# Random-feature attention with a gated layer: an account of engine times orders attention and its filling; row maxima in PSUM

## The chip, the cores and the metric

The kernel runs on one core of one Trainium2 chip. The metric is the device time of one execution in microseconds (us), median of several runs. The core's engines are named as in the profile: PE (matrix products; PEld are its weight loads), DVE (vector), ACT (scalar), POOL (GpSimd) and SP (here only a queue that issues DMAs). Each engine works through its own instructions in the order in which they stand in the program, and waits where an operand is not there yet.

## The reference

```
# q, k, v: [8, 8, 576, 64]; omega: [128, 64]
def phi(x):                                   # x = q or k, divided by 64 ** 0.25
    h = einsum('bhsd,md->bhsm', x, omega) - sum(x * x, -1, keepdims=True) / 2
    return exp(h - max(h, -1, keepdims=True)) / sqrt(128)
kv = einsum('bhsm,bhsd->bhmd', phi(k), v);  z = sum(phi(k), axis=2)
attn = einsum('bhsm,bhmd->bhsd', phi(q), kv) / (phi(q) . z + 1e-6)
x = attn, tokens by heads: [4608, 512]
out = (sigmoid(x @ w_gate) * (x @ w_val)) @ w_out      # d_ff = 1536; the three w are float64
```

## The kernel before

All products are float32. An operand of a large product is split into a rounded high part and the rest ("hi", "lo"), and three products of such parts stand for one (PE reads them as fp32r). The work has four stages.

**Attention** (`norms`, `projected`, `keys`, `queries`; L493 to L671). A unit `u` is two batches, 1152 tokens, 9 tiles of 128; there are 4 units, 4 pairs of heads `p`, and two halves `b` of a unit, one per batch. A task of `norms` loads token tiles (`nat`), squares them on ACT (`x2`) and sums them on DVE (`ss`, then `sq`). A task of `keys` or `queries` loads `raw`, splits it (ACT writes `hi`, POOL writes `lo`), and multiplies by omega on PE into a PSUM bank `pp`. DVE takes the row maxima `mx` (L552) and forms `hm` (L556). For keys, DVE forms `nb` (L574), ACT does the exponentials `kp` (L587), and PE sums `pkv` (L595) with the values `v`. For queries, DVE forms `sub` and `h` (L613, L615), PE transposes `h` into `pt`, ACT does `qp` (L628), PE multiplies by `kv` into `pn` (L638), DVE divides (`den`, `inv`, `x`: L643 to L649), PE transposes into `px` (L655), ACT copies to `xs` and issues the store of `xT` to DRAM (L663).

**First pass** (`first_pass`, L227): for each chunk of 512 tokens (the first in two halves), `load` brings `xr` from `xT`, ACT and POOL split it (`xe`), and PE makes gate and value of four of the twelve column tiles, 12 matmuls each (`gv`, L247); 80 such products ("wholes") in all. Once a chunk is split and its weights are there they depend on nothing in attention, so they are what PE can do while attention waits: the filling. **Conversion** (`from_float64`, `first_weights`, `convert_weights`; tiles `e`, `c`): six DVE instructions and one on POOL turn 512 columns of float64 weights into float32, 36 times; the later weights get four POOL subtractions and go back to DRAM (`w32`).

**Second pass** (`second_pass`, `gated`, L333): the other eight column tiles by a scheme of seven block products, into banks `gw`, 72 groups of 42 matmuls, three banks each. **Last** (L443): the product with w_out by the same scheme, into four banks `po` per block of 256 tokens, 18 blocks of 126 matmuls.

What sets the order before: the tasks are taken round robin by `attention` (L681), at most 6 at once. While the program is written, a counter gives attention 10 to 14 steps for each half product of the first pass, and one conversion step at a time from then on (L721 to L739). A scheduler of the framework then reorders all of it on every engine by its own estimate of when operands are there, except for what `pin` holds in place, which is the second pass and what belongs to it. PSUM has 8 banks: 6 with the tag `at` and 2 with `gv`; in the later stages `any_bank` takes three `at` and one `gv` in turn.

Of the kernel before, what the change touches and what calls it, by code (L numbers as in the profile page):

```python
# [45 lines left out]
AT_ONCE = 6  # L46
AHEAD = 8
EVERY = 32
FROM = 20
RATE = 14  # L50
FIRST = 10

RAWS, SPLITS, KPS, VS, HS, XS = 6, 5, 8, 3, 4, 3
# [13 lines left out]

def split(nc, hi, lo, x, lo_engine=None):

    nc.scalar.activation(out=hi, in_=x, func=AF.Copy)  # L70
    (lo_engine or nc.vector).tensor_tensor(out=lo, in0=x, in1=hi.bitcast(F32), op=ALU.subtract)  # L71


def from_float64(nc, t, a, bits):
# [3 lines left out]
    nc.vector.tensor_scalar(out=a, in0=hi, scalar1=0x7FFFFFFF, scalar2=None, op0=ALU.bitwise_and)  # L78

# [15 lines left out]
    x = t.bitcast(F32)
# [4 lines left out]
def attn_glu_kernel(ctx: ExitStack, tc, qT, kT, qn, kn, va, om, ident, w, out):  # L100
    nc = tc.nc
# [36 lines left out]
    def converted(cv, i):  # L138


        raw = [cv[:, (1 + h) * 2 * WP : (2 + h) * 2 * WP] for h in range(2)]
        for h in range(2):
            o = i + h * WP
            nc.sync.dma_start(out=raw[h].rearrange("p (n two) -> p n two", two=2), in_=w[:, o : o + WP, :])
        yield
        for h in range(2):
            from_float64(
                nc, cv[:, h * WP : (h + 1) * WP], cv[:, 6 * WP :],
                raw[h].rearrange("p (n two) -> p n two", two=2),
            )  # L150
            yield

    def first_weights(pool, tiles):

        for j in range(NE):
            cv = tiles(f"e{j}")
            ws[j] = wh, wl = [pool.tile([P, WE], F32R, name=f"{t}{j}") for t in ("wh", "wl")]
            steps = converted(cv, j * WE)
            next(steps)
            for i in range(2):  # L160
                next(steps)
                s = slice(i * WP, (i + 1) * WP)
                split(nc, wh[:, s], wl[:, s], cv[:, s].bitcast(F32), lo_engine=nc.gpsimd)
                yield

    def convert_weights(tiles, ns):

        for n in ns:
            cv = tiles(f"c{n}")
            for _ in converted(cv, NE * WE + n * 4 * Q):  # L170
                yield
# [9 lines left out]
            nc.sync.dma_start(out=w32[n], in_=f)  # L181
# [45 lines left out]
    def first_pass():  # L227


        def parts_of(o, n, at):  # L230
            raw = load(o, n)
            yield
# [5 lines left out]
        def product(i, j, o, n, x):  # L238
            name = f"gv{o}_{j}_{i}"
            gv = (any_bank(name) if late else bank("gv", name))[:, :n]  # L240
            wh, wl = ws[j]
            m = 0
            for k in range(KC):
                s = slice((i * KC + k) * P, (i * KC + k + 1) * P)
                xh, xl = x[k][:, 0], x[k][:, 1]
                for u, v in ((wl, xh), (wh, xl), (wh, xh)):
                    nc.tensor.matmul(gv, lhsT=u[:, s], rhs=v, start=(m == 0), stop=(m == 3 * KC - 1))  # L247
                    m += 1
            return gv
# [616 lines left out]
```

## Time and profile before

| | us |
|---|---|
| median of three runs (1235.72 to 1240.33) | 1237.9 |
| the profiled execution, whole | 1239.43 |
| its span, first to last instruction | 1237.6 |
| first matmul of the first pass (`gv`) starts at | 65.1 |
| last copy of attention (`xs`) starts at | 508.5 |
| last `gv` matmul starts at | 585.1 |
| second pass | 585 to 958 |
| last | 958 to 1238 |
| busy, of the span: PE, DVE, ACT, POOL | 1172.3, 864.5, 530.7, 542.7 |

The stages overlap in their beginnings. PE counts as busy from a matmul's start to its modelled end, and matmuls are pipelined, so that a busy PE may run well below its rate; how close they follow each other says more. PEclk in a row of the profile is the share of PE's full clock that it was granted.

### The profile page before, as it was taken

The page shows a single profiled execution, that of the slowest core. Times are in us where ns is not written, and L with a number is a line of the kernel's source. Part 1 is how long each engine was busy: PE and PEld are TensorE (multiplying, and loading weights), DVE is VectorE, ACT ScalarE, POOL GpSimd, SP SyncE. Part 2 cuts the span into 40 slices and gives each one's busy share as a digit, 9 for nine tenths or more (in the row PEclk, how much of TensorE's full clock was granted, in tenths as well). Part 3 has the DMA queues.
Part 4 walks back from the last instruction along what each step waited for, and adds up shares of the span by engine and source line. Part 5 has one row for each costly group of instructions (what it writes and reads, how often), then busy time and mean ns, then how long its engine had stood idle before and what let it go on. Part 6 is the DMA issues. An engine that isn't in the chain of part 4 may idle for free.

```text
span 1237.6 us, 23990 instructions
## 1 busy us (share of the span) xinstructions
PE 1172.3 (95%) x8828; PEld 1109.8 (90%) x8828; DVE 864.5 (70%) x1907; ACT 530.7 (43%) x1164; POOL 542.7 (44%) x599
## 2 busy tenths in 40 slices
PE   6798989999898999899899999999998899999998
PEld 5788978798887888788899999999998899999998
DVE  4889888999698866433566656666569777777773
ACT  5556755565455463342423322232325344343331
POOL 2454365556457552131466666666666211111110
PEclk7798989999899999899899999999999999999999
DMA  7667767786657641461432333323337676666662
GB/s 247 213 199 228 210 219 253 238 268 237 226 182 252 223 153 39 139 202 52 152 128 106 123 135 124 121 93 125 124 135 267 203 226 195 188 191 189 198 191 94
DMA packets 104950, 219.43 MB, mean 177 GB/s; under 512 B 11136, under 2 KB 42112, under 8 KB 103040
## 3 DMA queue, kind: packets, MB, share of 16 engines
q1 hardware_dynamic: 87984, 198.94, 48.5%
q10 hardware_dynamic: 16848, 18.95, 4.4%
q8 instruction: 70, 1.15, 0.4%
q14 instruction: 48, 0.39, 0.1%
HBM read 141.82 MB, written 76.02 MB: 176 GB/s over the span
## 4 chain that ended last, share of the span: by engine, by line
PE 71%; DVE 12%; issue 7%; DMA 5%; POOL 3%; ACT 1%; SPq 1%; ACTq 0%; DVEq 0%; POOLq 0%
PE gw L351 27%; PE po L465 20%; PE gv L247 10%; PE pkv L595 4%; PE pnq L638 4%; PE ptq L626 2%; DVE mxq L552 2%; DVE hq L615 1%; DMA xr<-xT 1%; DMA xT<-xsq 1%; DMA rawk<-kT 1%; POOL loq L71 1%; DVE hmq L556 1%; PE ppk L547 1%; POOL xe L71 1%
## 5 line engine op out<-in xcount | busy, mean ns | idle before, releaser
L351 PE MATMUL gw<-xl,u 128*128 128x256 f32 x3024 | 364.6, 283 | 6.9 <-ACT p L362 3.6
L351 PEld LDWEIGHTS gw<-xl,u 128*128 128x128 f32 x3024 | 363.5, 191 | 7.9 <-DVE u L331 3.9
L465 PE MATMUL po<-u,yh 128*128 128x256 f32 x1512 | 272.4, 283 | 0.0
L465 PEld LDWEIGHTS po<-u,yh 128*128 128x128 f32 x1512 | 234.8, 191 | 0.0
L465 PE MATMUL po<-u,yl 128*128 128x256 f32 x756 | 214.0, 283 | 3.3 <-DVE yl L71 3.3
L247 PE MATMUL gv<-xe,wh 128*128 128x512 f32 (+1 forms) x640 | 201.0, 388 | 2.1 <-POOL xe L71 2.1
L70 ACT ACTIVATE yh<-yr 128x896 fp32r<-128x896 f32 x108 | 100.2, 950 | 156.8 <-PE po L465 86.3
L465 PEld LDWEIGHTS po<-u,yl 128*128 128x128 f32 x756 | 144.3, 191 | 3.9 <-DVE yl L71 3.9
L247 PEld LDWEIGHTS gv<-xe,wh 128*128 128x128 f32 x640 | 117.3, 194 | 20.1 <-POOL xe L71 4.5
L71 POOL TENSOR_TENSOR yl<-yr,yh 128x896 fp32r<-128x896 f32 x17 | 38.0, 2232 | 215.3 <-PE po L465 139.9
L247 PE MATMUL gv<-xe,wl 128*128 128x512 f32 (+1 forms) x320 | 125.8, 394 | 2.7 <-POOL wl L71 1.6
L71 DVE TENSOR_TENSOR yl<-yr,yh 128x896 fp32r<-128x896 f32 x91 | 103.0, 1144 | 31.5 <-PE po L465 19.1
L331 DVE TENSOR_TENSOR u<-gw,p 128x256 f32<-128x256 f32 x144 | 60.7, 422 | 59.2 <-PE gw L351 51.1
L595 PE MATMUL pkv<-v,kpk 128*128 128x66 f32 x512 | 84.4, 290 | 13.3 <-ACT kpk L587 12.6
L595 PEld LDWEIGHTS pkv<-v,kpk 128*128 128x128 f32 x512 | 77.0, 209 | 21.5 <-ACT kpk L587 19.8
L71 POOL TENSOR_TENSOR lok<-rawk,hik 128x256 fp32r<-128x256 f32 (+1 forms) x80 | 55.5, 712 | 68.0 <-ACT hik L70 67.6
L456 DVE TENSOR_TENSOR yr<-yr 128x128 f32<-128x128 f32 x144 | 60.1, 451 | 35.3 <-DMA yr<-ye 34.8
L71 POOL TENSOR_TENSOR xe<-xr,xe 128x512 fp32r<-128x512 f32 (+1 forms) x40 | 49.1, 1244 | 74.2 <-ACT xe L70 62.4
L71 POOL TENSOR_TENSOR loq<-rawq,hiq 128x256 fp32r<-128x256 f32 (+1 forms) x80 | 56.5, 718 | 55.5 <-ACT hiq L70 54.7
L587 ACT ACTIVATE kpk<-ppk,nb 128x128 f32<-128x128 f32 x256 | 69.8, 393 | 17.4 <-DVE nb L574 17.1
L638 PEld LDWEIGHTS pnq<-kv,qpq 128*128 128x128 f32 (+1 forms) x640 | 70.5, 189 | 6.5 <-ACT qpq L628 4.3
L638 PE MATMUL pnq<-kv,qpq 128*128 128x66 f32 (+1 forms) x640 | 74.9, 273 | 1.4 <-ACT qpq L628 1.2
(108 smaller groups left out, 2166.6 us busy)
## 6 DMA issues: line engine op xcount, KB each, us to landing
yl<-yl SPq DMA_DIRECT2D x36, 896.0 KB, 3.8
yr<-yl SPq DMA_DIRECT2D x72, 448.0 KB, 3.5
xr<-xT SPq DMA_DIRECT2D x68, 256.0 KB, 4.7
c<-w SPq DMA_DIRECT2D x28, 512.0 KB, 5.1
w<-c SPq DMA_DIRECT2D x14, 1024.0 KB, 4.5
v<-va SPq DMA_DIRECT2D x32, 330.0 KB, 3.4
natk<-kn SPq DMA_DIRECT2D x36, 256.0 KB, 4.2
natq<-qn SPq DMA_DIRECT2D x36, 256.0 KB, 3.9
```

The source lines that it names most:

```text
L70: nc.scalar.activation(out=hi, in_=x, func=AF.Copy)
L71: (lo_engine or nc.vector).tensor_tensor(out=lo, in0=x, in1=hi.bitcast(F32), op=ALU.subtract)
L247: nc.tensor.matmul(gv, lhsT=u[:, s], rhs=v, start=(m == 0), stop=(m == 3 * KC - 1))
L331: return nc.vector.tensor_tensor(out=o, in0=a, in1=b, op=ALU.add)
L351: nc.tensor.matmul(o, lhsT=u[:, k, s], rhs=v[:, kc, :], start=(first and m == 0), stop=(m == 5), skip_group_check=not first,)
L456: nc.vector.tensor_tensor(out=raw[:, o], in0=raw[:, a], in1=raw[:, b], op=op)
L465: nc.tensor.matmul(o, lhsT=u[:, i, :], rhs=v[:, k, :], start=(j + m == 0 and n in (1, 6, 5, 4)), stop=(j == NPAIR - 1 and m == 2), skip_gr ...
L552: nc.vector.tensor_reduce(out=m.rearrange("p t h -> p (t h)"), in_=pp, axis=AX.X, op=ALU.max)
L587: nc.scalar.activation(out=kp[t][:, h, :], in_=pp[:, 2 * i + h, :], func=AF.Exp, bias=nb[:, t - t0, h : h + 1], scale=SCALE,)
L595: nc.tensor.matmul(pkv[:, h, :], lhsT=kp[b * MID + i][:, h, :], rhs=v[:, i, h, :], start=(i == 0), stop=(i == MID),)
L626: nc.tensor.transpose(out=pt[:, i, :], in_=h_sb[:, i, :], identity=id_sb)
L638: nc.tensor.matmul(pn[r, 2 * i + h, :], lhsT=qp[:, 2 * i + h, r], rhs=kvs[u, p, bb][:, h, :], start=True, stop=True,)
```

## The change

Only the stretch in which attention, the first pass and the conversions are mixed is written anew, and the bank tags. The arithmetic is the same.

1. `Clock` keeps, while the program is made, a time per engine and per tile: each instruction that is recorded moves its engine's time on by a fixed part and a part per element, a tile is due at its writer's end, a DMA's target 2.5 us after it is recorded. It also keeps apart the DVE instructions that read two SBUF operands (or run at double rate) and the POOL instructions, which it lets not overlap.
2. Every step of a task now says which engine it goes to and when its operands are due. `attention` records, in this order of preference: a step of ACT, DVE or POOL that is due; a conversion step, if DVE is free; a PE step of attention that has been due for 0.5 us; three matmuls of the first pass; a PE step that is just due; else it moves the account on. Older tasks go first. `fill` puts single conversion instructions between dependent small DVE instructions.
3. This stretch is written with `manual_schedule`, so that PE, DVE, ACT and POOL keep exactly the recorded order. SP's queue is still the framework's.
4. At most 62 of the 80 wholes are placed in this stretch (LEFT = 18).
5. `mx` and `hm` move from SBUF tiles to one PSUM bank, `small`; `at` keeps 5 banks, `gv` 2, also for the second pass and the last stage.
6. Tasks at once 6 to 7, `norms` up to 20 tasks ahead; buffers SPLITS 5 to 6, KPS 8 to 6, XS 3 to 4. The first four weight loads are issued first of all.

```diff
-AT_ONCE = 6
-AHEAD = 8
+AT_ONCE = 7
+AHEAD = 10
+LEFT = 18
+MARGIN = 0.5
+QUEUED = 2.0
-RAWS, SPLITS, KPS, VS, HS, XS = 6, 5, 8, 3, 4, 3
+RAWS, SPLITS, KPS, VS, HS, XS = 6, 6, 6, 3, 4, 4
+class Clock:
+    COST = {
+        "PE": (0.013, 1 / 2400, 0.27), "ACT": (0.1, 0.00082, 0.14), "DVE": (0.063, 0.001046, 0.12),
+        "POOL": (0.142, 0.00216, 0.13),
+    }
+    DMA = 2.5
...
+        if op == "dma_start":
+            if engine == "ACT":
+                self.at[engine] = max(self.at[engine], after) + 0.33
+            self.written[o] = max(self.at["PE"], after, self.used.get(o, 0.0)) + self.DMA
+            return
...
-    banks = {"at": 6, "gv": 2}
+    banks = {"at": 5, "gv": 2}
+    small = ps.tile([P, 2, SMALL, MID + 1, 2], F32, tag="small", bufs=1, name="small")
...
+    def conversions(pool, tiles):
+        ins = [j * WE for j in range(NE)] + [NE * WE + n * 4 * Q for n in range(N_LATE)]
+        following = loaded(tiles("c0"), ins[0])
...
+            yield "PE", max(there(*ws[j], x[0]), 0.0 if late else free_at("gv"))
             gv = (any_bank(name) if late else bank("gv", name))[:, :n]
...
+                if k < KC - 1 and not late:
+                    yield "PE", there(x[k + 1])
...
-            mx = pool.tile([P, MID + 1, 2], F32, tag="mx", bufs=4, name=f"mx{id_}")
+            slot = live[1] = (live[1] + 1) % SMALL
+            mx, hm = small[:, 0, slot], small[:, 1, slot, i0:i1]
+            yield "PE", lambda: max(there(sq, *(x for g in parts for x in g[2:4])), free_at("at", len(some)))
...
-            hm = pool.tile([P, MID + 1, 2], F32, tag="hm", bufs=4, name=f"hm{id_}")[:, i0:i1]
...
+        yield "PE", lambda: max(there(last_kp, v), free_at("at"))
         pkv = any_bank(f"pkv{u}_{p}_{b}")[:, : 2 * E].rearrange("p (h e) -> p h e", h=2)
...
+            a = next((a for a in side if when(a[3]) <= now + 0.2 and at[a[3][0]] <= now + QUEUED), None)
+            if a:
+                step(a)
+                continue
...
+            a = next((a for a in main if when(a[3]) + MARGIN <= now), None)
+            if a:
+                step(a)
+                continue
+            if gate[0] and when(gate[0]) <= now and whole[0] < 2 * NE * (NCH + 1) - LEFT:
+                gate[0] = next(gates)
+                continue
...
+            with tc.manual_schedule(engines={getattr(mybir.EngineType, e) for e in MANUAL}):
+                attention(pool, gates, conversions(early, tiles))
```

In the changed program every recorded instruction of the engines carries the line of the helper that records it, L154.

**The queue of SP at the start.** Before, the first keys and their token tiles come first (`rawk`, `natk`, then `v` and the tiles of the queries, `natq`):

```order
L114 DMA om_sb<-om 128x256
L519 DMA rawk_0_0_84<-kT 128x640
L499 DMA natk_0_87<-kn 128x512
L519 DMA rawk_1_0_91<-kT 128x640
L499 DMA natk_1_94<-kn 128x512
L499 DMA natk_2_99<-kn 128x512
```

and of the change:

```order
L154 DMA om_sb<-om 128x256
L154 DMA c_87<-w 128x1024 x2
L154 DMA c_90<-w 128x1024 x2
L154 DMA natk_0_97<-kn 128x512
L154 DMA natk_1_99<-kn 128x512
L154 DMA natk_2_101<-kn 128x512
L154 DMA rawk_0_0_103<-kT 128x640
L154 DMA rawk_1_0_105<-kT 128x640
```

The four loads of weights, 512 KB each, stand ahead of the first tile of keys.

**PE, the sums over the keys.** Before, at the second half of the first unit's keys (`pkv0_1_1` is unit 0, heads 1, half 1; `kmid` is the tile that both halves share, and long there; `kpk` are the new exponentials; the number at a name's end is the tile's):

```order
L595 MATMUL pkv0_1_1_1012<-v0_1_1_930,kmidk0_1_4_178 128x66
L595 MATMUL pkv0_0_1_1025<-v0_0_1_963,kmidk0_0_4_219 128x66
L247 MATMUL gv0_2_0_1070<-xe0_0_678,wl2_979 128x256
L247 MATMUL gv0_2_0_1070<-xe0_0_678,wh2_978 128x256 x2
L247 MATMUL gv0_2_0_1070<-xe0_1_681,wl2_979 128x256
L247 MATMUL gv0_2_0_1070<-xe0_1_681,wh2_978 128x256 x2
L247 MATMUL gv0_2_0_1070<-xe0_2_684,wl2_979 128x256
L595 MATMUL pkv0_1_1_1012<-v0_1_1_930,kpk0_1_5_934 128x66
```

and of the change:

```order
L154 MATMUL pxq0_3_0_912<-id_sb_69,xq0_3_0_846 128x128 x2
L154 MATMUL pxq0_1_2_922<-id_sb_69,xq0_1_2_885 128x128 x2
L154 MATMUL pkv0_1_1_945<-v0_1_1_801,kmidk0_1_4_289 128x66
L154 MATMUL pkv0_1_1_945<-v0_1_1_801,kpk0_1_5_805 128x66 x2
L154 MATMUL pkv0_1_1_945<-v0_1_1_801,kpk0_1_7_855 128x66 x2
L154 MATMUL pkv0_1_1_945<-v0_1_1_801,kmidk0_1_4_289 128x66
L154 MATMUL pkv0_1_1_945<-v0_1_1_801,kpk0_1_5_805 128x66 x2
L154 MATMUL pkv0_1_1_945<-v0_1_1_801,kpk0_1_7_855 128x66 x2
```

The sum stood open among products of the first pass, with its later matmuls waiting for exponentials in the middle of them; now it stands as one run, later. Over the whole program 180 recorded matmuls of attention stand ahead of the first `gv` before, and 295 after; behind the last matmul of attention stand 318 of the 960 `gv` matmuls before, and 210 after. (A recorded matmul of `pkv` or `pn` runs as two on the chip.)

**PE, a block's first matmuls in the last stage.** In square brackets stands the engine that an instruction waits for. Before, the fourth bank of a block, `po3`, is written without a wait (`u8` is the weight, `yl`, `yh` the split activations):

```order
L465 MATMUL po2_3_1_13815<-u8_12034,yl3_1_0_13826 128x256
L465 MATMUL po2_3_1_13815<-u8_12034,yh3_1_0_13825 128x256 x2
L465 MATMUL po2_3_1_13815<-u8_12034,yl3_1_0_13826 128x256
L465 MATMUL po2_3_1_13815<-u8_12034,yh3_1_0_13825 128x256 x2
L465 MATMUL po3_3_1_13816<-u8_12034,yl3_1_0_13826 128x256
L465 MATMUL po3_3_1_13816<-u8_12034,yh3_1_0_13825 128x256 x2
```

and of the change:

```order
L154 MATMUL po2_3_1_13595<-u8_11814,yl3_1_0_13606 128x256
L154 MATMUL po2_3_1_13595<-u8_11814,yh3_1_0_13605 128x256 x2
L154 MATMUL po2_3_1_13595<-u8_11814,yl3_1_0_13606 128x256
L154 MATMUL po2_3_1_13595<-u8_11814,yh3_1_0_13605 128x256 x2
L154 MATMUL po3_3_1_13596<-u8_11814,yl3_1_0_13606 128x256 [waits DVE_49]
L154 MATMUL po3_3_1_13596<-u8_11814,yh3_1_0_13605 128x256 x2
```

With 7 banks the fourth one is the first bank of the block before, which DVE may still read. The same wait is new at `po3` of 17 blocks, and in the second pass at the second or third bank of 71 of the 72 groups.

More of the change, by code (lines that the diff above doesn't have):

```diff
@@ L153, in first_weights @@
[L153 to L171, printed above, removed]
+            nc.sync.dma_start(
+                out=cv[:, (1 + h) * 2 * WP : (2 + h) * 2 * WP].rearrange("p (n two) -> p n two", two=2),
+                in_=w[:, o : o + WP, :],
+            )
@@ L248, in product, with begun @@
                     m += 1
+                if k < KC - 1 and not late:
+                    yield "PE", there(x[k + 1])
+            whole[0] += 1
             return gv
         chunks = [(0, Q), (Q, Q)] + [(c * NC, NC) for c in range(1, NCH)]
-        x = [t for t in parts_of(*chunks[0], keep) if t is not None]
+        def begun(o, n, at):
+            while not ready(o + n):
+                yield None
+            p = parts_of(o, n, at)
+            return next(p), p
+        raw, parts = yield from begun(*chunks[0], keep)
+        yield "ACT", there(raw)
+        x = list(parts)
         at, homes = keep, []
         for (o, n), after in zip(chunks, chunks[1:] + [None]):
-            ahead, parts = [], None
+            ahead, parts, raw = [], None, None
             for j in range(NE):
-                if after and parts is None and (j == NE - 1 or late):
+                if after and parts is None and ((j == NE - 1 and ready(sum(after))) or late):
                     if late:
@@ L280, in first_pass @@
                 nc.sync.dma_start(out=ye[j // 2, :, o // NC, j % 2, i : i + n // Q], in_=y[:, : n // Q])
-                yield
-            x = ahead + list(parts or ())
+                if late:
+                    yield "end", 0.0
+            if after and parts is None:
+                raw, parts = yield from begun(*after, at)
+            if parts:
+                if not late:
+                    yield "ACT", there(raw)
+                x = ahead
+                for t in parts:
+                    x.append(t)
     def operands(c):
@@ L525, in projected, with halved @@
         groups = GROUPS[name][b]
-        for some in (groups,) if name == "k" else [(g,) for g in groups]:
+        def halved(some):
             parts = []
+            while SPLITS - live[0] < len(some):
+                yield None
+            live[0] += len(some)
+            yield "ACT", there(raw)
             for tiles in some:
@@ L585, in keys @@
                     kp[t] = x[:, 2 * i : 2 * i + 2, :]
+                    yield "ACT", there(nb)
                     for h in range(2):
@@ new lines, in attention @@
+            late_by = made / total < sum(through) / (NP * U * T) / CONV_END or (gate[0] is None and made < 64)
+            alone = wants[0] and (wants[0][0] != "DVE" or not any(i <= max(now, at["DVE"]) < j - 0.1 for i, j in clock.pool))
+            if alone and when(wants[0]) <= max(now, at["DVE"]) + 0.2 and at["DVE"] <= now + (CONV_LATE if late_by else CONV_QUEUED):
+                made += 1
+                wants[0] = next(conv, None)
+                ended = wants[0] is None
+                continue
@@ L704, in ready @@
+        for _ in conv:
+            pass
     def ready(n):
```

348 lines of the change are left out of this document (257 added, 91 removed).

## The prediction

> **What bounds the kernel now.** I read the busy times by stage first (windows, in us: busy time and instructions of PE, PEld, DVE, ACT, POOL; granted clock; DMA).
>
> ```profile
> 0.00:65.00 65.00, 46.27 (x239) 43.53 (x240) 40.45 (x91) 34.98 (x95) 24.27 (x34) 0.76 0.70 232
> 65.00:95.00 30.00, 27.22 (x209) 25.75 (x209) 25.77 (x64) 17.76 (x49) 16.13 (x18) 0.94 0.57 186
> 65.00:508.00 443.00, 412.43 (x2980) 369.26 (x2980) 366.89 (x945) 246.31 (x682) 222.44 (x260) 0.96 0.61 204
> 515.00:585.00 70.00, 68.84 (x298) 55.47 (x298) 24.14 (x29) 26.48 (x41) 18.54 (x14) 1.00 0.47 154
> 585.00:958.00 373.00, 366.14 (x3040) 365.12 (x3039) 235.59 (x485) 119.53 (x222) 232.86 (x271) 0.99 0.37 135
> 958.00:1238.00 280.00, 271.65 (x2257) 270.83 (x2255) 196.75 (x358) 102.99 (x124) 44.57 (x22) 0.99 0.61 187
> ```
>
> PE looks full everywhere, but a matmul's busy time overlaps the next one's. So I read spacings from the timeline (start, length, operation, count) at full clock, and counts by kind for 0 to 585 us.
>
> ```profile
> 596.27 344.01 PE L351 MATMUL gw<-xl,u 128*128 128x256 f32 x2862 [3.57 <-ACT p L362]
> 499.27 1.90 PE L638 MATMUL pnq<-kv,qpq 128*128 128x66 f32 x16
> 562.37 0.63 PE L247 MATMUL gv<-xe,wh 128*128 128x512 f32 x2
> 563.07 0.63 PE L247 MATMUL gv<-xe,wh 128*128 128x512 f32 x2
> 21.77 1.91 PE L595 MATMUL pkv<-v,kpk 128*128 128x66 f32 x8
> L247 PE MATMUL gv<-xe,wh 128*128 128x512 f32 x511 | 173.9, 409 | 1.4 <-POOL xe L71 1.4
> L547 PE MATMUL ppk<-omH,lok 128*128 128x256 f32 x144 | 46.0, 320 | 10.0 <-POOL lok L71 10.0
> L595 PE MATMUL pkv<-v,kpk 128*128 128x66 f32 x512 | 84.4, 290 | 13.3 <-ACT kpk L587 12.6
> L638 PE MATMUL pnq<-kv,qpq 128*128 128x66 f32 x512 | 68.0, 283 | 1.2 <-ACT qpq L628 1.2
> L626 PE MATMUL ptq<-id_sb,hq 128*128 128x128 f32 x288 | 47.7, 286 | 11.9 <-DVE hq L615 7.9 <-DVE invq L647 1.7 <-ACT qpq L628 0.7
> ```
>
> The spacings: 344.01/2862 = 0.120 for 256 columns (0.117 without its small gaps), (1.90 - 0.27)/15 = 0.108 for float32 with 66 or 128, and 0.70/3 = 0.233 for 512. With 768 `gv` of 512 columns (511 `wh`, one record missing, and half as many `wl`) and 192 of 256 in the first chunk, six groups of 144 for `pp`, 640 each of `pkv` and `pnq`, 288 `pt` and 144 `px`, dense PE work up to 585 us is 179 + 22 + 101 + 139 + 31 + 16 = **488 us**. So 97 us are lost there. By the same spacings the windows hold 26.7 us of dense work in the first 65 (0.41), 387 in 65 to 508 (0.874: 56 lost), and 69.5 of the last 70. The second pass at 0.120 per matmul has almost nothing to give, the last stage likewise.
>
> The first 65 us are slow by latency and by the clock (0.76; the eight `pkv` at 21.77 follow each other at about 0.23 instead of 0.108). For 65 to 508 I read who PE waited for; where whole stretches are thin (dense 20.0 of 30 at 155 to 185, 21.2 at 305 to 335, 23.8 at 485 to 515, against 28.5 to 30 in good ones); and the chain and ACT's timeline in one of them.
>
> ```profile
> PE pkv L595 <- ACT kpk L587: 7.8, 9, 2.5
> PE ptq L626 <- DVE hq L615: 6.0, 10, 1.2
> PE pxq L655 <- DVE xq L649: 5.2, 6, 1.8
> ...
> 155.00:185.00 30.00, 26.23 (x159) 23.55 (x158) 23.83 (x62) 16.15 (x39) 17.87 (x21) 0.83 0.69 224
> 305.00:335.00 30.00, 26.81 (x164) 24.50 (x163) 19.31 (x52) 11.51 (x32) 12.93 (x16) 0.83 0.63 220
> 485.00:515.00 30.00, 27.73 (x172) 23.64 (x171) 14.27 (x46) 7.04 (x15) 0.00 (x0) 0.89 0.18 58
> ...
> 311.88 4.36 DMA xT<-xsq
> 316.31 3.55 DMA xr<-xT
> ...
> 319.88 0.63 ACT L70 ACTIVATE xe<-xr 128x512 fp32r<-128x512 f32 x1 [3.73 <-DMA xr<-xT]
> 320.41 2.16 ACT L587 ACTIVATE kpk<-ppk,nb 128x128 f32<-128x128 f32 x8
> ```
>
> In that stretch ACT stood before a chunk that was still on its way from DRAM, the exponentials queued behind it, PE ran out of work and its clock fell to 0.83. So the bound here is order: PE has enough to do in sum, and stands behind queues.
>
> **The change part by part.** *DVE's small instructions.* `hm`, `sub` and `nb` read two SBUF operands; `den` reads PSUM.
>
> ```profile
> L556 DVE SCALAR_TENSOR_TENSOR hmq<-mxq,sqq 128x4 f32<-128x4 f32 (+1 forms) x80 | 24.7, 320 | 0.0
> L613 DVE TENSOR_TENSOR subq<-sqq,hmq 128x4 f32<-128x4 f32 (+1 forms) x80 | 19.5, 254 | 0.0
> L643 DVE TENSOR_SCALAR denq<-pnq 128x4 f32<-128x4 f32 (+1 forms) x80 | 12.4, 156 | 36.5 <-PE pnq L638 35.8
> L556 DVE SCALAR_TENSOR_TENSOR hmk<-mxk,sqk 128x10 f32<-128x10 f32 (+1 forms) x32 | 11.3, 354 | 0.1
> L574 DVE SCALAR_TENSOR_TENSOR nb<-sqk,hmk 128x10 f32<-128x10 f32 (+1 forms) x32 | 10.3, 321 | 0.1
> ...
> L556 DVE SCALAR_TENSOR_TENSOR hmq<-mxq,sqq x80: 127/155/1247, 38.4 to 502.9; 128x4 f32<-128x4 f32 x64, 128x2 f32<-128x2 f32 x16
> ```
>
> Half of `hmq` take 155 ns and the longest 1247 (minimum, median, maximum). At `den`'s 156 ns the 224 instructions would take 35 of their 65.8 us: 31 us of DVE's 367 go. Bounds: 0, if these waits only change their place, and 31. Taken: 25, but hardly any of it lies on PE's path by itself; of PE's 11 us of waits for `hq` and `xq` I take 3.
>
> The Trainium skill, "SBUF — State Buffer", section "SBUF: two separate sides", says that DVE with two SBUF inputs and GpSimd exclude each other for a whole instruction; that agrees with the 1247 ns. Against the change speaks "Perfetto Trace Analysis", section "Optimizing Scalar/DVE Operations": about 60 ns of overhead per DVE instruction on SBUF, 125 on PSUM. By it 224 x 65 ns = 15 us would come back to DVE (an estimate from that page); the `den` row, 156 ns from PSUM beside 155, shows none of it, and the sum would not move, since DVE keeps slack.
>
> *The start.* First matmul and first filling:
>
> ```profile
> 8.49 0.58 PE L547 MATMUL ppk<-omH,lok 128*128 128x256 f32 x1 [8.49 <-POOL lok L71]
> L247 PE MATMUL gv<-xe,wl x320: 278/391/775, 65.1 to 584.7; 128*128 128x512 f32 x128, 128*128 128x256 f32 x32
> e<-w SPq DMA_DIRECT2D x8, 512.0 KB, 6.4
> ```
>
> Ahead of the first keys now stand 2.1 MB of weights. At the 232 GB/s of the first window they cost 9 us if all else waits, 0 if the queues share; I take 4, so PE starts at 12.5. Then 44.2 us of dense attention stand ahead of the first `gv` (295 recorded matmuls, by the spacings), where 26.8 stood before. At the pace of 65 to 95 us, 23.6 dense in 30 us (0.787), they end at 12.5 + 56 = 69. I take that pace, since seven tasks now run by due times; at the old 0.41 they would end at 108. The weights for the filling are converted earlier and are no limit there.
>
> *The middle.* All dense work ahead of attention's last matmul is 438.9 us (750 `gv` instead of 642), so 394.7 lie between. Before, 56 of 443 were lost. The three thin stretches brought up to 28.5 give 8.5 + 7.3 + 4.7 = 20.5, and they go because the filling now runs about 100 matmuls behind the tokens that are ready: the load of `xr` is no longer the last thing before its use. With the 3 from DVE: 387/(443 - 23.5) = 0.922, so 394.7/0.922 = 428. Bounds: 0.874 (452) and 0.97, the best 30 us stretches (407). Sum of moved DMAs: the same transfers; two in SP's order are earlier, none is added. Cover that may go: conversions now run to the end of attention, where DVE had room (14 of 30 us in the last thin stretch); it needs 367 - 25 us of 428, which fits.
>
> *The tail.* 210 `gv` instead of 318 behind attention: 49.0 dense, at the 69.5 of 70 seen there and the handover (74.0 of 76.5 from 508.5 on) 51 us. The loads of `u` (ten DMAs for the second pass) now share 51 us instead of 77; DMA is 0.47 busy there, so I put nothing on it.
>
> *The banks.* 71 groups and 17 blocks get a wait for DVE.
>
> ```profile
> 1036.56 0.37 ACT L473 ACTIVATE p1o<-po 128x256 f32<-128x256 f32 x1
> 1040.45 0.41 DVE L331 TENSOR_TENSOR o<-po,p1o 128x256 f32<-128x256 f32 x1
> ```
>
> `p1o` follows a block's sixth matmul of its final 21; `po3` of the next block comes 33 matmuls later, 3.6 us after `p1o` starts. DVE's last read of the bank ends 4.3 after it here, the worst of 17, with two near it; the others are in time. So 2 us, and 17 x 0.7 = 12 at most. In the second pass the wait costs 0 if DVE is as prompt as now, and at most one DVE addition (0.41) for each of 71 groups, 29. Taken: 2 in all. Nothing here can gain.
>
> *Sum*: 69 + 428 + 51 = 548 for the 585 us now, + 2: **35 us less**. The profiled execution was 1239.43 with a span of 1237.6; 1202.6 + 1.8 = 1204.4, and the median lies 1.5 under that execution: **1203**.
>
> **The rivals.** *The first stretch keeps its pace.* The order does not do what it says: with little filling the clock stays low. 44.2/0.41 = 108; 108 + 428 + 51 + 2 = 589, that is 1241, no change. For it: 0.76 of clock, and that the filling starts later in the order. Against: the row at 65 to 95 us, with only the 256-column filling of the first chunk in it, runs at 0.94. "TensorE: Matmul & The Clock Gate", Part 1, of the Trainium skill says that the gate opens after some 3.4 us of activity and closes on idleness; the rows with 0.76 and 0.83 agree in that thin stretches are slow ones, and by that rule either outcome feeds itself.
>
> *The account's DMAs are too fast* (slower than before). It puts a transfer at 2.5 us.
>
> ```profile
> xr<-xT SPq DMA_DIRECT2D x68, 256.0 KB, 4.7
> natk<-kn SPq DMA_DIRECT2D x36, 256.0 KB, 4.2
> xT<-xsq ACTq DMA_DIRECT2D x64, 128.0 KB, 2.8
> ```
>
> Store and load of a chunk take 7.5 where the account has 5. If ACT is led to `xe` too early, all of attention stands behind it as at 316 us, which cost 7.3 there. At eight chunks 58 us: 1203 + 58 = 1261. It takes five such stalls to eat the gain. Against it: the filling lies a chunk behind.
>
> *The banks cost their bounds*: 12 + 29 instead of 2, 1203 + 39 = 1242; it decides from about 0.4 us in each of 88 waits. "Perfetto Trace Analysis", section "Identifying Performance Opportunities", names repeating bubbles as the mark of too few buffers in PSUM; no row here shows them, and the second pass at 0.120 leaves none.
>
> *Better*: the start at 64, the middle at 0.97 (407), 51 behind: 522, and 1175.
>
> **How the numbers follow.** The sum 0.55; better 0.16; first stretch 0.13; early ACT 0.10; banks 0.06. The range goes from 1173 to 1242 and leaves out about 2 in 10, the far ends of the second and third rival and a better best. Beyond 0.5%, which is about what a measurement can tell from no change: faster 0.75 (the sum, better, and a part of the rivals), within it 0.13, slower 0.12.
>
> **What would show it.** Right: first `gv` near 69, last `xs` near 498, last `gv` near 549; dense work over 0.9 in the middle; `hm` and `sub` near 156 ns; `gw` at 0.120 per matmul. Wrong: ACT waiting for `xr` or `nat` for over 30 us in sum with PE idle behind it; a clock under 0.8 until 100 us; PE waiting for DVE at `gw` or `po3`; a POOL queue, full with the four `xe` of a chunk, that holds back `lo`.

## The result, and the profile after

The changed kernel takes **1228.8 us** (median of 8 runs, 1225.1 to 1232.9) where the kernel before takes 1237.4 (8 runs beside it, 1231.7 to 1241.2): ratio 0.9929, 95% interval 0.9905 to 0.9953. That is 8.5 us less, where 35 were forecast. The profiled execution took 1229.92, with a span of 1228.1. Medians and ratios in this document are of the fast runs; only one run is left out by this, of e9, with 1604 us at a granted clock of 0.66. Stage by stage, in its own times:

| stage (us; in brackets, behind the stage before) | before | forecast | measured |
|---|---|---|---|
| first matmul | 8.5 | 12.5 | 16.2 |
| first `gv` | 65.1 | 69 | 92.1 |
| last `xs` | 508.5 | 498 (428 behind the first `gv`) | 524.3 (432) |
| last `gv` | 585.1 | 549 (51) | 574.4 (50) |
| second pass and last stage | 652.5 | 654.5 | 653.7 |

The first fence gives three groups of the profile after (count, shortest, median and longest ns, first and last start); every recorded operation now has the line of the recorder, 154, so tiles are read instead of lines. The second gives its windows.

```profile
L154 PE MATMUL ppk<-omH,lok x144: 277/281/581, 16.2 to 435.8; 128*128 128x256 f32 x144
...
L154 PE MATMUL gv<-xe,wl x320: 277/393/774, 92.1 to 573.9; 128*128 128x512 f32 x128, 128*128 128x256 f32 x32
...
L154 ACT ACTIVATE xsq<-pxq x80: 256/385/459, 55.9 to 524.3; 128x256 f32<-128x256 f32 x64, 128x128 f32<-128x128 f32 x16
```

```profile
0.00:65.00 65.00, 39.33 (x222) 36.98 (x222) 38.39 (x85) 38.13 (x104) 17.29 (x28) 0.82 0.74 242
65.00:95.00 30.00, 25.43 (x189) 23.59 (x190) 24.01 (x65) 18.66 (x57) 13.81 (x18) 0.89 0.71 227
...
215.00:245.00 30.00, 30.00 (x179) 26.80 (x178) 20.42 (x53) 14.78 (x42) 11.47 (x17) 0.84 0.69 224
275.00:305.00 30.00, 30.00 (x223) 27.95 (x222) 25.34 (x63) 17.96 (x53) 14.26 (x18) 1.00 0.72 229
```

By the spacings of the prediction, from 275 to 305 the windows hold 30 us of dense work in 30, and from 215 to 245, where the clock is 0.84, 26. Of the 26 us that the sum was off, 23 stand in one place: the first `gv` at 92 instead of 69. All behind it is within 4 us of the forecast. The thin stretches of the kernel before at 305 and 485 us are filled now (30.3 and 27.8 dense in 30, by the same counts). The third one, at 155, is not: 21.2, where it had 20.0. And from 125 to 155 the windows hold 23.2, where the kernel before had 28.4. So what is thin now lies ahead of 245 us.

The place of the maxima shows as forecast (by form: busy us, mean ns):

```profile
L154 DVE SCALAR_TENSOR_TENSOR small<-small,sqq 128x4 f32<-128x4 f32 x64 | 10.7, 167 | 1.3
L154 DVE TENSOR_TENSOR subq<-sqq,small 128x4 f32<-128x4 f32 x64 | 10.1, 158 | 2.2
```

The first is `hm`: 167 ns where it took 293, `sub` 158 where it took 235. And PE's waits from 600 us on (what waited, for what; us in total, times, longest) show what the bank given away costs: the row for `o`, which the kernel before does not have, has 4.5 us.

```profile
PE po L154 <- DVE o L154: 4.5, 4, 1.5
PE po L154 <- DVE yl L154: 3.8, 3, 2.2
PE gw L154 <- DVE u L154: 3.3, 3, 1.4
```

### The profile page after: what moved, and what is told of

It is laid out like the page before. It is cut to its first block, busy times and chain, and to the rows that moved or that the text cites. A ratio compares the mean times of both kernels' runs of the same rounds, so it can differ in the third digit from the quotient of the medians.

```text
span 1228.1 us, 23968 instructions
## 1 busy us (share of the span) xinstructions
PE 1160.7 (95%) x8828; PEld 1102.8 (90%) x8828; DVE 864.8 (70%) x1907; ACT 525.3 (43%) x1164; POOL 539.4 (44%) x599
## 4 chain that ended last, share of the span: by engine, by line
PE 73%; DVE 10%; DMA 6%; issue 5%; POOL 2%; ACT 2%; SPq 1%; DVEq 0%; ACTq 0%; POOLq 0%
PE gw L154 27%; PE po L154 18%; PE gv L154 11%; PE pkv L154 4%; PE pnq L154 4%; PE ppq L154 3%; PE ppk L154 3%; DVE small L154 2%; PE ptq L154 2%; DVE c L154 2%; DMA yr<-ye 1%; DVE yl L154 1%; DMA xT<-xsq 1%; SPq L154 1%; DMA xr<-xT 1%
## 5 line engine op out<-in xcount | busy, mean ns | idle before, releaser
L154 PE MATMUL gw<-xl,u 128*128 128x256 f32 x3024 | 362.5, 282 | 4.1 <-DVE u L154 3.7
L154 PEld LDWEIGHTS gw<-xl,u 128*128 128x128 f32 x3024 | 361.1, 190 | 5.4 <-DVE u L154 4.7
L154 PE MATMUL po<-u,yh 128*128 128x256 f32 x1512 | 272.6, 283 | 0.0
L154 PEld LDWEIGHTS po<-u,yh 128*128 128x128 f32 x1512 | 234.9, 191 | 0.0
L154 PE MATMUL po<-u,yl 128*128 128x256 f32 x756 | 214.5, 284 | 8.2 <-DVE o L154 4.5
L154 PE MATMUL gv<-xe,wh 128*128 128x512 f32 (+1 forms) x640 | 186.6, 375 | 2.6 <-POOL xe L154 1.7
L154 ACT ACTIVATE yh<-yr 128x896 fp32r<-128x896 f32 x108 | 100.7, 952 | 162.6 <-PE po L154 99.4
L154 PEld LDWEIGHTS po<-u,yl 128*128 128x128 f32 x756 | 144.3, 191 | 9.7 <-DVE o L154 5.3
L154 POOL TENSOR_TENSOR c<-c 128x256 f32<-128x256 f32 (+1 forms) x92 | 88.7, 976 | 111.8 <-DVE c L154 53.6
L154 PEld LDWEIGHTS gv<-xe,wh 128*128 128x128 f32 x640 | 117.5, 192 | 21.7 <-POOL xe L154 5.2
L154 POOL TENSOR_TENSOR yl<-yr,yh 128x896 fp32r<-128x896 f32 x17 | 39.1, 2299 | 220.3 <-PE po L154 142.2
L154 POOL TENSOR_TENSOR yl<-yl,gl 128x256 f32<-128x256 f32 x106 | 96.7, 913 | 80.6 <-issue 39.1
L154 PE MATMUL gv<-xe,wl 128*128 128x512 f32 (+1 forms) x320 | 129.2, 404 | 1.7 <-ACT ge L154 0.9
L154 DVE TENSOR_TENSOR yl<-yr,yh 128x896 fp32r<-128x896 f32 x91 | 101.4, 1123 | 35.7 <-PE po L154 20.7
L154 DVE TENSOR_TENSOR u<-gw,p 128x256 f32<-128x256 f32 x144 | 60.7, 422 | 58.4 <-PE gw L154 50.4
L154 POOL TENSOR_TENSOR loq<-rawq,hiq 128x256 fp32r<-128x256 f32 (+1 forms) x80 | 57.5, 729 | 77.1 <-ACT hiq L154 73.7
L154 DVE TENSOR_TENSOR yr<-yr 128x128 f32<-128x128 f32 x144 | 62.2, 467 | 36.7 <-DMA yr<-ye 36.2
L154 DVE TENSOR_SCALAR c<-c 128x512 uint32<-128x512 uint32 (+1 forms) x144 | 78.3, 544 | 10.7 <-DMA c<-w 5.2
L154 PEld LDWEIGHTS pnq<-kv,qpq 128*128 128x128 f32 (+1 forms) x640 | 70.8, 187 | 12.3 <-ACT qpq L154 6.1
L154 PE MATMUL pnq<-kv,qpq 128*128 128x66 f32 (+1 forms) x640 | 75.3, 270 | 4.3 <-ACT qpq L154 3.5
L154 POOL TENSOR_TENSOR lok<-rawk,hik 128x256 fp32r<-128x256 f32 (+1 forms) x80 | 56.6, 731 | 50.0 <-ACT hik L154 47.5
L154 PE MATMUL pkv<-v,kpk 128*128 128x66 f32 x512 | 75.2, 295 | 1.8 <-ACT kpk L154 1.1
```

Source lines behind the costliest of these rows:

```text
L154: i = f(*a, **k)
```

## The experiments

All start from the changed kernel, unless they say otherwise. The ratio is to the kernel before, run beside them; the changed kernel's is 0.9929 (0.9905 to 0.9953). The pace is the dense attention ahead of the first `gv` (from PE's order) over the time from the first key matmul to the first `gv`; the clock is that granted from 0 to 585 us. In every profile it reads 1.00 up to the first change that was recorded, also where the spacings say half speed (in the changed kernel 0.21 us for 256 columns from 16.2 to 19.8, in e4 until 22.3), so that clocks counted from 0 on come out somewhat too high.

| run | time, us | ratio, 95% interval | first key matmul | first `gv` | pace | clock |
|---|---|---|---|---|---|---|
| before | 1237.4 | 1 | 8.5 | 65.1 | 0.47 | 0.94 |
| changed | 1228.8 | 0.9929 | 16.2 | 92.1 | 0.58 | 0.96 |
| e1 later keys held back | 1254.7 | 1.0148 (1.0117-1.0179) | 16.6 | 84.0 | 0.52 | 0.93 |
| e2 first keys early | 1221.4 | 0.9886 (0.9849-0.9923) | 9.5 | 87.8 | 0.55 | 0.96 |
| e3 clock held | 1217.8 | 0.9860 (0.9815-0.9905) | 18.2 | 86.3 | 0.65 | 0.98 |
| e4 maxima in SBUF | 1246.3 | 1.0072 (1.0038-1.0106) | 16.6 | 78.4 | 0.69 | 0.95 |
| e5 same, order kept | 1241.1 | 1.0023 (0.9998-1.0048) | 16.4 | 89.3 | 0.61 | 0.95 |
| e6 transfers at 4.5 us | 1255.7 | 1.0142 (1.0101-1.0182) | 19.0 | 103.4 | 0.50 | 0.93 |
| e7 order free but PE's | 1281.9 | 1.0353 (1.0299-1.0408) | 16.3 | 110.1 | 0.47 | 0.90 |
| e8 = e2 and e3 | **1214.0** | 0.9805 (0.9766-0.9844) | 16.9 | 82.5 | 0.65 | 0.98 |
| e9 half of e2: keys | 1221.7 | 0.9879 (0.9842-0.9915) | 13.3 | 90.1 | 0.56 | 0.95 |
| e10 half of e2: weights | 1234.0 | 0.9981 (0.9959-1.0004) | 17.7 | 97.0 | 0.58 | 0.96 |
| e11 nine tasks | 1243.6 | 1.0040 (1.0006-1.0075) | 17.6 | 90.3 | 0.65 | 0.95 |
| e12 five tasks | 1292.6 | 1.0437 (1.0396-1.0477) | 16.2 | 84.7 | 0.47 | 0.89 |
| e13 e8, shorter lead | 1217.4 | 0.9842 (0.9800-0.9884) | 9.2 | 85.2 | 0.56 | 0.97 |
| e14 e13, thinner | 1220.0 | 0.9860 (0.9822-0.9899) | 8.7 | 85.6 | 0.56 | 0.96 |

**e1, is too much attention put ahead of the first filling?**

```diff
-if name[0][0] != "n" and done.issuperset(needs) and ...
+if name[0][0] != "n" and (ready(Q) or name[1] == name[-1] == 0) and done.issuperset(needs) and ...
```

> Until the first 256 tokens of attention are through, only the first half of the first batch pair may be begun, as in the kernel before; all else as changed. In PE's order 34.9 us of dense attention stand ahead of the first gv where 44.2 stood. Theory (the account pulls later keys ahead of the first tokens, and the filling comes too late): at the pace of 0.58 that the changed kernel shows there, the first gv starts near 76 us instead of 92, and the end comes 6 to 10 us earlier, about 1219 to 1223. Rival (PE's work is only moved, what is late is latency and clock): the first gv comes earlier all the same, but the time stays within 1225 to 1233.

Both were wrong: the first `gv` came 8 us earlier, and the kernel lost 26. The windows of e1 show where (columns as in the prediction: busy time and instructions of PE, PEld, DVE, ACT, POOL; granted clock; DMA):

```profile
95.00:125.00 30.00, 24.58 (x151) 23.21 (x150) 21.98 (x57) 18.03 (x56) 11.18 (x17) 0.72 0.59 184
125.00:155.00 30.00, 27.54 (x187) 25.99 (x186) 17.68 (x48) 13.01 (x43) 9.58 (x12) 0.76 0.35 116
```

The changed kernel has 219 and 208 matmuls there, e1 151 and 187, at a clock of 0.72 and 0.76. It looks as if what was not begun early is missing behind; since the whole order changed, that is not shown. What e1 does show is that an earlier first `gv` alone does not make the kernel faster.

**e2, e9 and e10, what keeps the first keys.** The chain of the changed kernel's first 20 us (start, length, what):

```profile
3.06 6.99 DMA natk<-kn
10.07 0.64 ACT x2k L154
10.72 2.96 DMA natk<-kn
13.77 0.63 ACT x2k L154
14.44 0.63 ACT x2k L154
15.46 0.74 POOL lok L154
16.23 3.77 PE ppk L154 x16
```

The keys' own load is not in it. Their split stands behind five squares on ACT, the last of them on a load that waits for a buffer, and the program's order is now binding. e9 takes that away for the first keys (the first piece below; they then wait for their squares behind their matmuls), e10 issues the weights' first loads later (the second piece), e2 does both:

```diff
-while (name, u, b) not in sqs:
-    yield None
+if u or p or b or name == "q":
+    while (name, u, b) not in sqs:
+        yield None
 parts = yield from halved(todo[0])
...
-wants, gate = [next(conv)], [next(gates)]
+wants, gate = [("DVE", 0.0)], [next(gates)]
```

> The first keys are split and multiplied before their squares are there, and the first weight loads are issued behind the first loads of the attention. Theory (the start was lost to what stands ahead of the first keys): the first matmul at 8 to 10 us instead of 16.2, the first gv about 7 us earlier, near 85, the time 5 to 8 us lower, 1221 to 1224. Rival (the squares and norms behind them set the first stretch anyway): the first matmul moves but the first gv stays within 3 us of 92 and the time within 1226 to 1232.

> The first half of e2 alone: the first keys are split and multiplied before their squares are there; the weights stay ahead of them on SP's queue. Theory (the weights' loads cost about 4 us and the wait behind the squares the rest): the first matmul at 12 to 13 us, the time between e2's and the changed kernel's, 1223 to 1227. Rival (all 7 us are the squares): the first matmul within 1 us of e2's 9.5 and the time at 1219 to 1223.

> The second half of e2 alone: the first weight loads are issued behind the first loads of the attention; the first keys still wait for their squares. Theory: the first natk lands about 2 us after its issue sooner and the first matmul comes at 12 to 14 us, the time 1224 to 1228. Rival (the weights share the queues and cost nothing): first matmul within 1 us of 16.2, time 1226 to 1232.

The same group of e9, and then of e2:

```profile
L154 PE MATMUL ppk<-omH,lok x144: 276/286/582, 13.3 to 431.9; 128*128 128x256 f32 x144
```

```profile
L154 PE MATMUL ppk<-omH,lok x144: 276/286/580, 9.5 to 429.1; 128*128 128x256 f32 x144
```

So behind the squares 2.9 us are lost (16.2 to 13.3), and once the squares are out of the way, to the weights 3.8 (13.3 to 9.5), nearly as e9's theory had it. With the squares in place, moving the weights brings no such gain: in e10 the first matmul comes at 17.7, later than the 16.2 of the changed kernel, against both of its expectations, since the second `natk` then takes 8.0 us instead of 3.0. e2's time is what its theory said, its first `gv` is not (87.8 for 85). And e2 and e9 cannot be told apart in time (0.9886 and 0.9879), though PE starts 3.8 us earlier in e2, while e10 rather costs, by 0.9981 against 0.9929. So PE's start alone does not set the first stretch. Nor is the gain of e2 and e9 all from there: of the 7.7 us by which e9's last `gv` matmul starts earlier, only 2.0 lie ahead of the first `gv`. The first keys' new place also changes the order behind it (252 `gv` are then left behind attention, not 210), and what of the gain is due to that was not separated.

**e3, the clock.**

```diff
+def busy(n):
+    for _ in range(n):
+        raw_pe.matmul(junk[:, : 2 * M], lhsT=omH[:, :P], rhs=omH, start=True, stop=True)
+busy(70)
...
 t, _, a = min(rest, key=lambda x: x[:2])
+if not whole[0] and not clock.written.get("gv_began") and t > now:
+    busy(int((t - now) / 0.2))
```

> Matmuls of no use (into a bank of the filling that nobody reads yet) stand on PE from the start, 70 of them, and in the gaps that the account sees ahead of the first gv. Theory (the low granted clock is what makes the first stretch slow): the half-speed time before the first gv falls from about 30 us to under 10, the first gv starts near 78 and the time falls by 8 to 12 us, to 1217 to 1221. Rival (the latency of the other engines bounds the stretch, the clock only follows): first gv between 88 and 95, time within 1226 to 1233.

The windows of e3, and PE's two costliest groups until its first `gv` (line 904 is the added matmul):

```profile
0.00:65.00 65.00, 57.70 (x454) 55.43 (x454) 42.39 (x94) 40.62 (x110) 17.47 (x28) 1.00 0.80 260
65.00:95.00 30.00, 28.03 (x239) 26.73 (x239) 25.12 (x70) 20.44 (x64) 16.28 (x21) 1.00 0.69 219
```

```profile
L904 PE MATMUL junk<-omH 128*128 128x256 f32 x224 | 33.0, 298 | 3.6 <-ACT omH L154 3.6
L154 PE MATMUL pkv<-v,kpk 128*128 128x66 f32 x112 | 15.4, 276 | 0.6 <-ACT qpq L154 0.4
```

The clock is 1.00 where it was 0.82 and 0.89, and the time falls by 11 us, as the theory had it. Yet the first `gv` moves by 6 only, to 86.3, nearer to the rival's 88 than to the theory's 78, although PE was given 224 x 0.117 = 26 us of useless work on top. Of the 224, 107 run ahead of the first keys, which start at 18.2 for it; the other 117, 14 us, fit between the first keys and the first `gv`. So PE has time to spare in this stretch even at full clock: the clock is one loss, and the larger part of the wait is for something else. That this is the chain of each task over ACT, DVE and POOL is what the next two runs were to test.

**e11 and e12, the tasks at once** (`AT_ONCE` 9 with three of keys and five of queries, and 5, for 7).

> Nine tasks of attention may run at once instead of seven (three of keys, five of queries); 47.2 us of dense attention now stand ahead of the first gv. Theory (in the first stretch each task waits for its own chain over the engines, so the pace grows with the tasks at once): pace 0.65 or more, first gv at 89 or earlier, time 1222 to 1228. Rival (DVE, ACT or the banks set the pace, not the tasks): pace 0.58 as before, first gv near 97, time 1228 to 1236.

> Five tasks at once instead of seven; 32.2 us of dense attention stand ahead of the first gv. Theory (pace by tasks at once): pace near 0.42, first gv about 92 again, and the time rises by over 5 us, 1234 or more, since less attention is then begun. Rival: pace 0.58, first gv near 72, time within 1224 to 1232.

The pace goes with the tasks: 0.47, 0.58 and 0.65 for 5, 7 and 9. As for the pace, e11's theory holds, and five tasks came out at 0.47 for the 0.42 of e12's; the first `gv` came later than e11's theory had it (90.3 for 89) and earlier than e12's (84.7 for 92). But the tasks are not all: e4, with seven tasks and a sixth bank for attention, has the highest pace of all, 0.69, and its first `gv` at 78.4. In the changed kernel PE stands 5.8 us in front of `ppk` in this stretch with nothing that the profile shows it waiting for; in e4 that row is gone. So the sixth bank, which the prediction priced only for the later stages, is a rival here. It is open, since e4's whole order differs. The time does not follow the pace: with nine tasks the first `gv` comes 2 us earlier and the end 15 us later, with thin stretches further on, as in this window of e11 (147 matmuls where the changed kernel has 223):

```profile
275.00:305.00 30.00, 26.82 (x147) 24.57 (x146) 19.06 (x46) 15.22 (x43) 13.94 (x16) 0.77 0.64 213
```

**e4 and e5, the place of the maxima.** In both:

```diff
-mx, hm = small[:, 0, slot], small[:, 1, slot, i0:i1]
+mx = pool.tile([P, MID + 1, 2], F32, tag="mx", bufs=12, name=f"mx{id0}")
+hm = pool.tile([P, MID + 1, 2], F32, tag="hm", bufs=12, name=f"hm{id0}")[:, i0:i1]
```

e4 has six banks for attention again, and its account knows of SBUF; in e5 the account is left as it was, with five banks.

> The row maxima and what is made of them lie in SBUF again, and attention has its sixth bank back; the account and its order stay. Theory of the prediction (these instructions are short in PSUM, but hardly on PE's path): hm, sub and nb go from 160 to 170 ns to a mean of 250 to 320, DVE's busy time rises by 25 us up to 585, and the time rises by about 3 us, 1230 to 1234. Rival (the bank that was given away costs more than the shorter instructions bring): faster by 4 us or more, 1225 or less, with the waits for a bank in the second pass and the last stage gone.

> As e4, maxima in SBUF, but the account still counts them as PSUM and attention keeps five banks: the order on PE, DVE, ACT and POOL is the changed kernel's, row for row, and only the place of the maxima differs. Theory (e4 lost its 17 us through another order, and the place by itself is worth little): 1228 to 1234, with hm, sub and nb at 250 to 320 ns. Rival (DVE standing before GpSimd at these instructions is what costs): 1240 to 1247, like e4.

The two groups of e5 that answer to those shown above:

```profile
L154 DVE TENSOR_TENSOR subq<-sqq,hmq 128x4 f32<-128x4 f32 x64 | 27.7, 433 | 2.2
...
L154 DVE SCALAR_TENSOR_TENSOR hmq<-mxq,sqq 128x4 f32<-128x4 f32 x64 | 17.4, 271 | 1.3
```

With the same order the place by itself is worth 12 us of time (1.0023 against 0.9929): e5's 1241.1 lies in its rival's range, 7 us above the theory's. `hm`, `sub` and `nb` together take 36.7 us in the changed kernel and 76.9 in e5; of these 40 us, 9 came back at the conversions (`c<-c`, 132.2 us against 123.3). From the first `gv` to the last `xs` e5 takes 443.7 us, the changed kernel 432.2, so the gain lies in the middle. e4 fits neither of its expectations: slower, as the theory said, but by 17 us. Its second pass and last stage take 651.0 us, the changed kernel's 653.7. But in the runs with five banks the same stretch takes between 650.4 (e12) and 659.7 (e1), so what the sixth bank is worth there cannot be told from this; PE's waits for `o` are gone with it. Why e4's first `gv` comes at 78.4 and its end as late, with 12 us of dense work in the 30 from 515, is open: two things differ in it, the banks and the order.

**e6 and e7, the account and its order** (`DMA = 4.5`; `MANUAL = {"PE"}`).

> The account's figure for a transfer is 4.5 us instead of 2.5, nearer to the 3.5 to 4.7 that the trace shows from issue to landing. Theory (the figure matters little, since the filling lies behind the tokens that are there): 1224 to 1233, the first gv within 5 us of 92. Rival (the account leads ACT to transfers that are still on their way): ACT's waits for DMA shrink, and the time falls by 5 us or more, 1223 or less.

> Only PE keeps the order in which the program was written; on DVE, ACT and POOL the framework may move instructions again. Theory (the middle gained because all four engines work the account's order): the middle from the first gv to the last xs loses most of its 20 us, 1240 to 1250. Rival (PE's order alone carries the gain): 1225 to 1233.

Both expectations for e6 fell: the figure matters, and the truer one costs 27 us. A window of e6, and three waits in it, PE's longest among them:

```profile
35.00:65.00 30.00, 17.09 (x97) 16.11 (x97) 17.39 (x38) 13.45 (x41) 8.38 (x11) 0.67 0.45 146
```

```profile
POOL lok L154 <- ACT hik L154: 9.4, 2, 8.0
...
PE ppq L154 <- POOL loq L154: 8.1, 1, 8.1
ACT x2k L154 <- DMA natk<-kn: 7.4, 1, 7.4
```

ACT stands 7.4 us before a token tile that is still on its way, POOL's split behind ACT, PE 8.1 us behind POOL, and the clock is 0.67. It is the stall that the longer figure was to avoid. Why the account chooses so with this figure is open. e7 loses 53 us, more than either expectation: with PE fixed and the others free, PE's longest waits from 90 to 220 us are for `hq`, which it hardly waited for (0.6 us in the changed kernel):

```profile
PE ptq L154 <- DVE hq L154: 11.0, 4, 5.8
```

So the order of all four engines is worth much once PE's is fixed; what the framework would make of it with PE free too was not tried.

**e8, e13 and e14, both at once.**

> e2 and e3 together. Theory (two separate losses, a late first matmul and a low clock): the gains add in part, since matmuls of no use shrink with the gaps; the first gv at 78 to 84, the half-speed time before it under 6 us, 1207 to 1214. Rival (both take the same loss out): 1215 to 1221.

> As e8, but 33 matmuls of no use stand ahead of the first keys instead of 93, so that they end near 9 us, when the first keys are split; in e8 the first keys were ready at 9.1 and PE began them at 16.9. Theory (a late first matmul and a low clock are two losses): the first matmul of the keys at 9 to 10.5, the first gv 4 to 7 us earlier than e8's 82.5, the time 1207 to 1211. Rival (past the clock the chain over the other engines sets the stretch): first gv within 3 us of 82.5, time 1212 to 1217.

> As e13, with 67 matmuls of no use in all instead of 149. Theory (few are enough to hold the clock): half-speed time before the first gv under 5 us and the time as e13 within 3 us. Rival (thinner ones let the clock fall in the gaps): over 15 us of half speed before the first gv, time 1214 to 1222 like e2.

PE's timeline in e8 shows that its first keys stood behind the useless matmuls, which e13 then made fewer (`busy(10)`):

```profile
3.57 13.45 PE L907 MATMUL junk<-omH 128*128 128x256 f32 x93 [3.57 <-ACT omH L154]
16.86 0.28 PE L154 MATMUL ppk<-omH,lok 128*128 128x256 f32 x1
```

e8 came out as its theory had it, at the edge (1214, first `gv` 82.5). But in e13 the keys start at 9.2, and nothing comes of it: the next keys' `lok` is late, PE stands for 4.8 us, and the clock falls after all, to 0.50 from 20 to 28 us.

```profile
11.10 2.68 PE L907 MATMUL junk<-omH 128*128 128x256 f32 x21
18.59 0.58 PE L154 MATMUL ppk<-omH,lok 128*128 128x256 f32 x1 [4.81 <-POOL lok L154]
```

By its first `gv` (85.2) e13 is as its rival said, by its time (1217.4) at the rival's edge. But the clock was not held in e13, 0.92 up to the first `gv` against 1.00 in e8. So an earlier start and a lower clock stand against each other there, and what an earlier start is worth with the clock held was not tested. e14 (67 useless matmuls in all instead of 149) lies in both of its ranges for the time, but its clock up to the first `gv` is 0.86, no better than e2's 0.88 without any: so few do not hold it, as its rival said. e8 beats both kernels, the changed one by 15 us; e3, e13 and e14 are not told apart from it with certainty.

## Why the prediction was wrong, point by point

- **The start: the step that failed.** "At the pace of 65 to 95 us, 23.6 dense in 30 us (0.787), they end at 12.5 + 56 = 69." That row was of a stretch with filling in it, and I used it for attention alone. The same 30 us of the kernel before, by form:

```profile
L247 PE MATMUL gv<-xe,wh 128*128 128x256 f32 x40 | 9.0, 313 | 0.8 <-POOL xe L71 0.8
L247 PE MATMUL gv<-xe,wl 128*128 128x256 f32 x20 | 6.3, 329 | 1.1 <-ACT xe L70 1.1
```

  60 `gv` of 256 columns are 7.0 us; attention had 16.6 in 30, 0.55. With that, 12.5 + 44.2/0.55 = 93 (92.1 measured), and the sum becomes 93 + 428 + 51 + 2 = 574 for 585: 11 us less instead of 35, and 1227 instead of 1203. That it comes so near is in part luck, since PE began later (16.2) and the pace behind that was higher (0.58). The terms of the miss of 23 us are: first matmul 16.2 for 12.5, 4 us, most of it the first keys' wait behind the squares (2.9 in e9), for which the sum had no term; the rest of the stretch 19, of which 6 are the clock (as much as e3 moved the first `gv`) and 13 are left at full clock. What these 13 wait for is not settled: more tasks raise the pace (e11, e12), and so may a sixth bank (e4).
- **The rival on the first stretch** was right in kind: the filling begins later and the clock stays low, 0.84 in 95 us. It was wrong in size. Its 0.41 counts from 0, with the 8.5 us in which PE had not begun; counted so, the changed kernel has 44.2/92.1 = 0.48, and counted from the first key matmul, 0.58 for 0.47. The result lies between this rival (1241) and the sum (1203), so its 0.13 was too low a chance.
- **The middle: right in sum, wrong in its parts, and so by luck.** 394.7 us of dense work took 432, forecast 428. Of the three thin stretches that were to be filled, two were, and a good one ahead of them became thin. I put 3 us on the shorter maxima and 20.5 on the order. e5 gives 11.5 to the place of the maxima; order and the rest have 8 (452 at the old fill, 443.7 in e5). The 452 is an estimate, the forecast's own bound. "Hardly any of it lies on PE's path by itself" was the error. In the same order, e5 has 190 matmuls from 95 to 125 us, at a clock of 0.87, where the changed kernel has 219 at 1.00:

```profile
95.00:125.00 30.00, 25.65 (x190) 24.04 (x189) 27.15 (x67) 17.78 (x56) 13.90 (x17) 0.87 0.54 170
```

- **DVE's durations: right.** 156 ns were forecast, 158 and 167 measured. The Trainium skill, "SBUF — State Buffer", section "SBUF: two separate sides", agrees with both runs: `sub` with two SBUF inputs took 160 to 1280 ns in e5, with one from PSUM 156 to 161. Of the rule that spoke against the change, 65 ns more for an instruction on PSUM, the rows show little: the median of `hm` is 155 ns before, 164 in e5 and 168 in PSUM, that of `sub` 164 in e5 and 158 in PSUM.
- **The tail: right.** 49.0 of dense work took 50, forecast 51.
- **The banks: right that they cost little there.** 1.2 us more for the second pass and the last stage, forecast 2; differences of this size are within what the stretch varies by from run to run (650.4 to 659.7 with five banks). The rival with 39 us is refuted. What the bank is worth in the first stretch had no term, and stays open (e4).
- **"The account's DMAs are too fast"**: refuted as put. From 90 to 530 us ACT waits for `xr` once, 3.2 us, where five stalls of 7.3 were needed; and the truer figure makes the kernel slower (e6).
- **A sum in "better"**: 64 + 407 + 51 leaves out the 2 us for the banks; by the forecast's own terms it is 1177, not 1175.

## What to carry to other kernels

A pace read from a stretch holds for its mix only: take the filling out of it before using it for a stretch that has none. Where PE has much to spare and still is late, ask how many chains run at once, how many banks they have and what they wait for; an earlier start of PE alone need not help then (e2 against e9). Before a change of data's place is costed at next to nothing because another engine has slack, ask whether the instructions stand ahead of something that PE waits for, and whether its clock falls meanwhile.

## What the runs showed of the hardware

**The clock makes a small gap expensive.** In the runs of the table the time goes, roughly, with the clock granted up to 585 us: 0.98 in e3 and e8, 0.96 and 1229 in the changed kernel, 0.90 and 0.89 in e7 and e12 with 1282 and 1293. It is no close rule: at 0.95 stand 1222 (e9) and 1246 (e4). One place where small gaps are followed by half speed, on PE's timeline in the changed kernel (start, length; in brackets the idle time ahead):

```profile
210.76 0.49 PE L154 MATMUL gv<-xe,wl 128*128 128x512 f32 x1 [0.26 <-ACT xe L154]
212.11 0.73 PE L154 MATMUL gv<-xe,wh 128*128 128x512 f32 x2 [0.86 <-DVE denq L154]
213.34 0.66 PE L154 MATMUL ptq<-id_sb,hq 128*128 128x128 f32 x4 [0.50 <-ACT kpk L154]
...
215.80 1.92 PE L154 MATMUL pkv<-v,kpk 128*128 128x66 f32 x8
...
221.03 0.41 PE L154 MATMUL ppk<-omH,lok 128*128 128x256 f32 x1
...
225.45 0.28 PE L154 MATMUL ppq<-omL,hiq 128*128 128x256 f32 x1
```

Gaps of 1.6 us in sum were followed by some 10 us in which a matmul of 256 columns took 0.41 us instead of 0.28, and the next followed after 0.21 instead of 0.12. Matmuls of 66 and 128 columns stand among these gaps too, so the gaps need not be the only cause.

**Long runs of `pkv` did not bring the clock back.** In the changed kernel, for 4.5 us from 25.19 and again for 5 us from 30.87, `pkv` follow each other without a gap, and all eight of a group still take 1.9, where the group takes 1.0 at full clock. In the kernel before they do so from 17.1 to 26.2. The first two lines are from there; the other three are of e12, with narrow matmuls alone (66 or 128 columns), in its first line mostly `pkv`, in the last two `ptq`, `pnq` and a few `pxq`:

```profile
20.20:23.20 3.00, 3.00 (x16) 3.00 (x16) 0.75 (x2) 2.93 (x10) 0.00 (x0) 0.50 1.01 401
23.20:26.20 3.00, 3.00 (x15) 2.85 (x14) 2.32 (x6) 0.13 (x1) 0.00 (x0) 0.50 0.87 316
113.60:124.10 10.50, 10.48 (x60) 10.19 (x60) 2.66 (x10) 4.66 (x17) 1.74 (x3) 0.50 0.13 36
567.00:570.60 3.60, 3.60 (x20) 3.37 (x19) 2.20 (x7) 1.19 (x2) 0.00 (x0) 0.53 0.00 0
570.60:572.00 1.40, 1.40 (x15) 1.40 (x14) 0.94 (x4) 0.00 (x0) 0.00 (x0) 1.00 0.00 0
```

So 9 and 10 us of PE without a gap left the clock at half, while in e12 some 3.6 us of `ptq` and `pnq` from 567 on brought it back. Matmuls of 256 columns brought it back in 3.6 us from 16.23, in about 3 from 37.37, and in 6.1 at the start of the kernel before (8.5 to 14.6). The Trainium skill, "TensorE: Matmul & The Clock Gate", Part 1, gives about 3.4 us of activity; the wide ones agree with it roughly, the runs of `pkv` do not, and what share of a matmul counts as activity was not measured by itself.
